# Four edits to a planned attention-and-FFN kernel: the first q in two parts, new delays in the planner, a second recursion level in one more block, and the last stores on two queues

## The chip, the cores and the metric

The kernel runs on one core of a Trainium2 chip. The core has five engines that run their own instruction streams in order: TensorE (PE; its weight loads are listed as PEld), VectorE (DVE), ScalarE (ACT), GpSimd (POOL) and SyncE (SP, which here only issues DMAs). They meet through semaphores. A DMA is issued by a queue on SP or ACT and its data is moved by the core's 16 DMA engines. The metric is device microseconds for one execution, lower is better. Before the change three runs gave a median of 1555.18 us, from 1553.32 to 1555.87.

## The reference

Two blocks in a row, all in float32 but for the FFN's weights, which arrive as float64:

```python
# attention: q, k, v are (batch 8, heads 12, seq 448, head_dim 64)
q_n, k_n = rmsnorm(q, g_q), rmsnorm(k, g_k)      # x / sqrt(mean(x*x) + 1e-6) * g
attn = softmax(q_n @ k_n.T / sqrt(64))
x = (attn @ v)  ->  reshaped to (3584, 768)      # token rows, heads side by side
# FFN: w_a, w_b are (768, 1536), w_out is (1536, 768)
out = ((x @ w_a) * (x @ w_b)) @ w_out            # (3584, 768)
```

## The kernel before

**Attention.** The work goes in 24 "couples" (`p`), each four heads of one batch entry, two and two on the halves of the 128 partitions. For a couple the kernel loads q, k and v (`loads`, L422; each as two DMAs of 224 KB on SP, one for each half), squares q and k on ScalarE (L456), sums the squares on VectorE (L458), scales them (L462) and takes the power -0.5 on GpSimd (L464), multiplies q by its root (`apply`, L468, tile `qn`), and turns k and q with TensorE transposes into one PSUM tile each (L494), which ScalarE copies out (L499 for k, L501 for q, times the gains). Then, over seven key blocks `j`, it makes scores (L515), exponentials (L521, two instructions a block, with k's root as the scale) and values (L537). The sum of exponentials is made by TensorE for the first five couples (L573) and by VectorE and GpSimd for the others (L551). Its reciprocal goes out to DRAM and back to be spread (`few`, `inv`, `rec`), and VectorE multiplies it in (L644).

**FFN.** The batch is taken in four blocks of two entries (`beta` 0 to 3). Each of the three products is done in Strassen's form with seven products in place of eight (the program's seven factors of a weight tile, `st`). The first two FFN products are `quarter_products` (L984, PSUM tile `pq`), the last one `last_product`, which handles pairs of 128-token tiles: three pairs in an even block, four in an odd one, and for each of seven products `f`, in the order 0, 1, 2, 4, 3, 5, 6, one TensorE product per pair (L726, tile `po`, 384 columns wide). In the fourth block alone (`ONCE = NB - 1`), and for five of the seven `f` (`TWICE`), two pairs at a time are done with a second level of the same recursion instead (`inner_products`): VectorE makes four sums of the left side (tile `Si`, L877), seven products of 192 columns go into five PSUM banks named a, b, d, g, e (L901), and small VectorE instructions of 192 or 384 columns put them together (L936 to L959). The right side's four extra factors are computed by VectorE in the second block (`inner_factors`, `MAKE = 1`, L840, tile `tk`), stored to DRAM (`kept_t`), and loaded again by `stream_inner` (tile `ti`, L856) into buffers that attention used: the four `ET` buffers, or the two of v and the one each of q and k. That load waits until the last couple has ended. Output rows are stored by `store` (L1056), two DMAs of 96 KB for 128 rows, all on SP; quarters of the second level first live in tiles `oi`, which take buffers of the nine-buffer pool `x`.

**Weights.** The float64 weights come in as words (`hraw`, `lraw`; `factors`, `rounding`, L379 loads on ACT) and are rounded to float32 by one ScalarE instruction (L271) and six VectorE ones, from which the seven factors are made, kept in DRAM, and loaded again for each later block (`stream`, L413 and L415). The first weight load is planned after the first k has arrived.

**What sets the order.** The class `Plan` collects every step with an engine, a cost in us, a priority key (smaller goes first), and what it reads and writes; tiles have a number of buffers. `run` simulates the engines with these costs, takes at each moment the ready step with the smallest key, and emits the instructions in that order. So each engine's program order is the planner's, and at run time an engine waits in that order. A step's result is available to another engine `LAG` = 0.1 us after its planned end. A DMA costs its size at 300 KB per us on one shared lane plus 2 us. TensorE has eight filler steps of warm-up (`warm`, L1073, 64 records in all) with the largest key: they run when nothing else is ready.

## Time and profile before

The profiled execution took 1556.43 us, of which 1554.5 us are the span from its first to its last instruction. Matmuls in float32 are recorded as two instructions each.

| quantity | value |
|---|---|
| median of three runs | 1555.18 us |
| profiled execution, its span | 1556.43 us, 1554.5 us |
| TensorE busy | 1515.1 us, 97% of the span |
| VectorE, ScalarE, GpSimd busy | 767.6, 399.3, 314.1 us |
| HBM read and written | 160.83 MB, 41.85 MB |
| quarter products L984 | 763.4 us by summed durations |
| last product, first level, L726 | 204.8 us (from hT) and 105.5 us (from fin) |

The stages stand one after the other on the time axis: attention of the first two blocks up to 236 us, with the rounding of the weights and the start of the FFN mixed in; the FFN of the first block from 236; attention in bursts around 394 to 522 and 755 to 882; and from 1139 to 1163 the last couples. The last product of the third block runs from 1172.4 to 1253.7, that of the fourth from 1443.1 to 1547.1. In the table of stretches a row gives the length, then for each engine its busy time and number of records, the clock granted to TensorE as a share of full speed, the share of time that the DMA engines were busy, and GB/s. The chain of waits is followed back from the last instruction; each piece is named by what it was waiting on or doing.

### The profile page before, as it was taken

To read this page: it belongs to the slowest core of one execution; us is meant where nothing else is said; L and a number is where in the kernel's file an instruction comes from. 1 tells how busy PE (TensorE), PEld (TensorE's weight loads), DVE (VectorE), ACT (ScalarE), POOL (GpSimd) and SP (SyncE) were. 2 spreads that over 40 slices of the span, in tenths; PEclk is the share of its full clock that TensorE was granted. 3 is DMA by queue.
4 is the path that set the end of the run, shared out by engine and by line. 5 is a ranking of instruction groups with operands and counts; after the bars stand their busy time and mean duration, and the time that the engine had idled before them with its cause. 6 is when DMAs were issued, how large, how long until landed. Compare 5 with 4: busy or idle time off the path is not lost.

```text
span 1554.5 us, 17614 instructions
## 1 busy us (share of the span) xinstructions
PE 1515.1 (97%) x6894; PEld 811.3 (52%) x6894; DVE 767.6 (49%) x1088; ACT 399.3 (26%) x647; POOL 314.1 (20%) x166
## 2 busy tenths in 40 slices
PE   8998999999999999999999999999999999999998
PEld 6554344555444555555444455555545555555796
DVE  4887869888786412222376532222135212222583
ACT  4767761111567200000456400000040000000000
POOL 2426442111255200011244400001110001000000
PEclk9999999999999999999999999999999999999999
DMA  8798445554535551212246445221324432222343
GB/s 238 223 264 247 97 104 181 184 196 152 161 110 126 143 164 71 107 71 102 78 107 167 107 149 169 77 101 71 107 74 139 130 124 104 75 88 84 117 137 105
DMA packets 122527, 204.09 MB, mean 131 GB/s; under 512 B 57156, under 2 KB 105540, under 8 KB 112708
## 3 DMA queue, kind: packets, MB, share of 16 engines
q1 hardware_dynamic: 94692, 149.80, 32.9%
q10 hardware_dynamic: 27744, 53.09, 9.8%
q8 instruction: 56, 0.92, 0.3%
q14 instruction: 35, 0.29, 0.1%
HBM read 160.83 MB, written 41.85 MB: 130 GB/s over the span
## 4 chain that ended last, share of the span: by engine, by line
PE 88%; DMA 5%; DVE 3%; ACT 3%; issue 1%; SPq 0%; POOL 0%; ACTq 0%; DVEq 0%; POOLq 0%
PE pq L984 49%; PE po L726 19%; PE o L537 6%; PE sc L515 6%; PE pt L494 2%; PE su L573 2%; ACT ET L521 2%; PE g L901 1%; DMA k_sb<-in_k_dram 1%; DMA q_sb<-in_q_dram 1%; PE a L901 1%; DMA rec<-inv 1%; PE warm L1073 1%; DMA hraw<-in_moe_w_out_dram 1%; PE b L901 1%
## 5 line engine op out<-in xcount | busy, mean ns | idle before, releaser
L984 PE MATMUL pq<-x,st 128*128 128x448 f32 x2016 | 763.4, 540 | 0.0
L984 PEld LDWEIGHTS pq<-x,st 128*128 128x128 f32 x2016 | 381.2, 190 | 378.6 <-issue 370.1
L521 ACT ACTIVATE ET<-sc,ms 128x448 f32<-128x448 f32 x336 | 192.6, 634 | 91.6 <-PE sc L515 67.1
L726 PE MATMUL po<-st,hT 128*128 128x384 f32 x624 | 204.8, 487 | 0.0
L515 PE MATMUL sc<-qkT 64*64 64x448 f32 x1344 | 176.7, 546 | 18.7 <-ACT ET L521 10.5
L537 PE MATMUL o<-ET,v_sb 64*64 64x448 f32 x1344 | 185.7, 551 | 8.1 <-ACT ET L521 7.5
L464 POOL TENSOR_TENSOR ms<-ms,expo 128x14 f32<-128x14 f32 x48 | 146.0, 3046 | 206.4 <-DVE ms L462 201.8
L1032 POOL TENSOR_TENSOR hT<-hT,t 128x448 f32<-128x448 f32 x24 | 28.7, 1197 | 745.9 <-DVE t L1030 743.7
L726 PEld LDWEIGHTS po<-st,hT 128*128 128x128 f32 x624 | 117.9, 190 | 84.7 <-issue 3.6
L1006 ACT COPY hT<-pq 128x448 f32<-128x448 f32 x24 | 12.8, 532 | 436.1 <-PE pq L984 436.1
L515 PEld LDWEIGHTS sc<-qkT 64*64 64x64 f32 x1344 | 58.5, 133 | 95.6 <-issue 35.0
L551 POOL TENSOR_TENSOR sum<-sum,ET 128x896 f32<-128x896 f32 x38 | 81.4, 2141 | 127.2 <-ACT ET L521 84.5
L726 PE MATMUL po<-st,fin 128*128 128x384 f32 x312 | 105.5, 490 | 0.0
L537 PEld LDWEIGHTS o<-ET,v_sb 64*64 64x64 f32 x1344 | 60.6, 134 | 84.9 <-issue 37.5
L726 PEld LDWEIGHTS po<-st,fin 128*128 128x128 f32 x312 | 58.3, 190 | 46.6 <-issue 8.5
L551 DVE TENSOR_TENSOR sum<-sum,ET 128x896 f32<-128x896 f32 x57 | 62.3, 1094 | 38.4 <-POOL sum L551 33.2
L746 DVE TENSOR_TENSOR o_sb<-fin,po 128x384 f32<-128x384 f32 x44 | 24.4, 554 | 112.7 <-PE po L726 108.6
L1044 POOL TENSOR_TENSOR hT<-hT,t 128x448 f32<-128x448 f32 x48 | 57.8, 1206 | 51.1 <-DVE t L1041 47.5
L458 DVE TENSOR_REDUCE ms<-sq 128x14 f32<-128x896 f32 x48 | 51.8, 1078 | 24.8 <-ACT sq L456 24.7
L1037 DVE TENSOR_TENSOR hT<-U,pq 128x448 f32<-128x448 f32 x48 | 29.8, 621 | 66.2 <-PE pq L984 66.2
L1041 DVE TENSOR_TENSOR t<-U,pq 128x448 f32<-128x448 f32 x48 | 29.7, 619 | 61.6 <-PE pq L984 59.3
L1009 ACT COPY t<-pq 128x448 f32<-128x448 f32 x24 | 12.8, 533 | 176.0 <-PE pq L984 176.0
(109 smaller groups left out, 1141.7 us busy)
## 6 DMA issues: line engine op xcount, KB each, us to landing
st<-kept SPq DMA_DIRECT2D x36, 1344.0 KB
st<-kept_o SPq DMA_DIRECT2D x28, 1152.0 KB
kept<-st ACTq DMA_DIRECT2D x12, 1344.0 KB
q_sb<-in_q_dram SPq DMA_DIRECT2D x48, 224.0 KB
k_sb<-in_k_dram SPq DMA_DIRECT2D x48, 224.0 KB
v_sb<-in_v_dram SPq DMA_DIRECT2D x48, 224.0 KB
rec<-inv SPq DMA_DIRECT2D x48, 224.0 KB
lraw<-in_moe_w_a_dram ACTq DMA_DIRECT2D x12, 768.0 KB
```

What stands on the lines that cost most here:

```text
L458: op("DVE", 1.1, key, lambda: nc.vector.tensor_reduce(rs[p][:, s], xs["sq", nm, p], AX, ALU.add), [sq], [f"{ms}/{nm}"])
L464: lambda: nc.gpsimd.tensor_tensor(msf(), msf(), expo[:, 0:2 * NT * (b - a)], ALU.pow), [], names)
L494: nc.tensor.transpose(t[:, j * P:(j + 1) * P], x[:, j].rearrange("p h d -> p (h d)"), ident)
L515: nc.tensor.matmul(t[low_high[w], e, 0:S], lhsT=qkTs[p][low_high[e], 1, j * P + w * D:j * P + (w + 1) * D], rhs=qkTs[p][low_high[e], 0, w ...
L521: nc.scalar.activation(E[:, e], scs[p, j][:, e, 0:S], AF.Exp, scale=rs[p][:, 1, 2 * j + e:2 * j + e + 1])
L537: nc.tensor.matmul(os_[p][low_high[e], w, 0:S], lhsT=xs["v", p][low_high[w], e, j * D:(j + 1) * D], rhs=ETs[p, j][low_high[w], e], start=( ...
L551: two[e].tensor_tensor(sums[p], sums[p] if j > 1 else ETs[p, 0], ETs[p, j], ALU.add)
L573: nc.tensor.matmul(sus[p][w][low_high[e], :], lhsT=ones[low_high[w], :], rhs=x[low_high[w], e], start=first, stop=last)
L726: nc.tensor.matmul(held["po"][:, 0:HALF], lhsT=a[0]()[:, c], rhs=sts[beta, 12 + place_of[f]][:, c], start=(c == 0), stop=(c == MH - 1))
L901: nc.tensor.matmul(held[bank], lhsT=x()[:, c], rhs=y(c), start=(start and c == 0), stop=(stop and c == MI - 1), skip_group_check=True)
L984: nc.tensor.matmul(banks[bank][:, 0:S], lhsT=sts[at][:, f, c * P:(c + 1) * P], rhs=quads[x][:, c], start=(start and c == 0), stop=(stop an ...
L1044: lambda i=i, n=n, nm=nm: two[TIMES].tensor_tensor(C(i, n), C(i, n), held[nm], ALU.mult), [t], [hp[i]],
```

## The change

1. *First q in two parts.* `begin_first`, called ahead of all else, allocates the first q tile and loads its second half from ACT's queue; the planned load then issues only the first half on SP. `prepare_first` replaces q's part of `normalize` for couple 0: squares, sums, scaling, power and `apply` are done for four of the seven 64-wide groups and then for three. The turn and the take of q are split alike, and the power for k is split in two, on which the first four and the last three key blocks' exponentials wait separately.
2. *Delays.* `LAG` is 0.05 us, and 0.22 us where the producer is TensorE.
3. *Second level in the third block.* `TWICE` becomes a table: all seven `f` in block `NB - 2`, the five as before in `NB - 1`; `ONCE` is `NB - 2`. The extra factors are made for all seven `f`. In the third block the pairs 0 and 1 are one group and pair 2 stays at the first level; pairs that stay alone are now issued ahead of the groups. With `ONCE` lower, the third block's FFN steps are listed after the last couple's, and its N sums are made by quarter as hT gets ready.
4. *The tail.* In the very last group (fourth block, `f` = 6, second group) product e goes ahead of the last g; the last product goes to a bank of its own, h, and the quarter is summed in two steps. For `f` = 6 of the fourth block each quarter row's two stores go to SP and ACT in turn.

```diff
-    LAG = 0.1
+    LAG, LAG_PE = 0.05, 0.22
...
-                    ready[u] = max(ready[u], end[x] + (self.LAG if ops[u][0] != e else 0.0))
+                    ready[u] = max(ready[u], end[x] + ((self.LAG if e != "PE" else self.LAG_PE) if ops[u][0] != e else 0.0))
...
-        TWICE = (1, 2, 3, 4, 6)
+        TWICE = {NB - 2: (0, 1, 2, 3, 4, 5, 6), NB - 1: (1, 2, 3, 4, 6)}
         MAKE = 1
-        ONCE = NB - 1
+        ONCE = NB - 2
...
+        FIRST = "q", 0
+        PARTS = slice(0, NT // 2 + 1), slice(NT // 2 + 1, NT)
+
+        def begin_first():
+            x = xs[FIRST] = ld.tile([P, 2, NT * D], FP32, tag="q", name="q_sb", bufs=1)
+            nc.scalar.dma_start(x[low_high[1]], q[0, 2:4].rearrange("h (p j) d -> p h (j d)", j=NT))
+
+        def prepare_first():
+            ms, key, sq = tile_of("ms0", "ms", 3), -NORM, tile_of("sqq0", "sq", 1)
...
+            for c in range(2):
+                n = PARTS[c].stop - PARTS[c].start
...
+                op("ACT", 0.1 + 0.13 * n, key, square, ["q0"], [f"{sq}/{c}"], new=[sq] if c == 0 else [])
+                op("DVE", 0.1 + 0.145 * n, key, lambda c=c, r=r: nc.vector.tensor_reduce(
...
+                op("POOL", 0.4 + 0.32 * n, key, lambda c=c, r=r, n=n: nc.gpsimd.tensor_tensor(
...
+                op("DVE", 0.1 + 0.145 * n, key, apply, [f"{ms}/q{c}", "q0"], [f"{qn}/{c}"], new=[qn] if c == 0 else [], lock=True)
...
+                        op("PE", 0.11 * m, key, turn_part, [f"qn0/{c}"], [f"{pt}/{c}"], new=[pt] if c == 0 else [], mode="full")
+                        op("ACT", 0.1 + 0.145 * m, key, take_part, [f"{pt}/{c}", "gain"], [f"{qkT}/0"])
...
-            op("ACT", 1.12, p, exps, [sc, f"ms{p}/k"], [E], new=[E])
+            op("ACT", 1.12, p, exps, [sc, f"ms{p}/k" if p else f"ms0/k{int(j >= PARTS[1].start)}"], [E], new=[E])
...
-                if beta == MAKE and f in TWICE:
+                if beta == MAKE:
                     inner_factors(beta, f)
-                if beta >= ONCE and f in TWICE:
+                if f in TWICE.get(beta, ()):
                     stream_inner(beta, f)
...
-                twice = groups if f in TWICE else []
+                twice = groups if f in TWICE.get(beta, ()) else []
+                for t in pairs if not twice else alone:
+                    product(t, f, a(t), plain(t, base, to))
                 for g in twice:
                     inner_products(beta, key + place_of[f], f, g, a, base, to, acc, (c_, U_), out_place)
-                for t in pairs if not twice else alone:
-                    product(t, f, a(t), plain(t, base, to))
...
+            third = lambda: product("e", s(3), b_quarter(1, 1), [f"{S_}/3", st], True, True)
+            last = beta == NB - 1 and f == 6 and group[0]
+            if last:
+                third()
+            product("g", s(2), b_made(2), [f"{S_}/2", f"ti{beta}.{f}.2"], True, bool(last))
...
+            if last:
+
+                w = write(1, 0)
+                add(0.36, lambda: V.tensor_tensor(dest(1, 0), part(1), held["g"], ALU.add), [g, f"{t_}/1"], **w)
+                home_of["h"] = "mm", 2
+                bank_of["h"] = tile_of(f"h_{id_}", "mm", 2)
+            product("h" if last else "g", a11, b_made(3), nx1 + [f"ti{beta}.{f}.3"], bool(last), True)
...
+                if beta == NB - 1 and f == 6:
+
+                    op("ACT", 1.0, -1, lambda x=x, t=t: store(out_place(t, to[0]), to[1], o_of[x], (nc.sync, nc.scalar)), [o_[x]], [],
+                       kb=197, dmas=2)
+                    continue
...
-                nc.sync.dma_start(rows[j][p0:p0 + n, x * HALF:(x + 1) * HALF], o_sb[at:at + n])
+                queues[0].dma_start(rows[j][p0:p0 + n, x * HALF:(x + 1) * HALF], o_sb[at:at + n])
+                queues.reverse()
...
         with tc.manual_schedule():
+            begin_first()
             setup()
             plan.run()
```

## The prediction

> **What bounds the kernel now.** I read four views in this order: the table of engines, a table of stretches of the span, the chain of waits, and the rows of the last twelve microseconds. First the engine table and the stretches (columns: length, then busy time and count for PE, PEld, DVE, ACT, POOL, then granted TensorE clock, DMA share, GB/s).
>
> ```profile
> PE 1515.1 (97%) x6894; PEld 811.3 (52%) x6894; DVE 767.6 (49%) x1088; ACT 399.3 (26%) x647; POOL 314.1 (20%) x166
> ```
>
> ```profile
> 15.00:40.00 25.00, 20.86 (x178) 12.24 (x182) 13.96 (x16) 14.10 (x20) 6.57 (x2) 0.86 0.91 293
> 40.00:80.00 40.00, 36.82 (x355) 23.08 (x347) 34.03 (x41) 28.51 (x46) 17.08 (x6) 0.96 0.81 225
> 80.00:120.00 40.00, 36.24 (x345) 19.75 (x337) 33.61 (x40) 29.02 (x45) 8.61 (x3) 1.00 0.98 267
> 120.00:160.00 40.00, 34.52 (x304) 16.73 (x302) 31.41 (x39) 29.52 (x49) 27.93 (x10) 1.00 0.72 216
> 882.00:962.00 80.00, 80.00 (x249) 47.10 (x248) 31.62 (x58) 0.00 (x0) 0.05 (x1) 1.00 0.52 164
> 1173.00:1254.00 81.00, 81.00 (x253) 47.69 (x252) 31.02 (x48) 1.44 (x3) 1.13 (x1) 1.00 0.43 137
> 1459.00:1517.00 58.00, 56.00 (x334) 53.73 (x333) 44.69 (x102) 2.65 (x9) 0.00 (x0) 1.00 0.51 156
> ```
>
> TensorE is the bound. It is without a gap where only FFN work is left (882 to 962, 1173 to 1254), and idle almost only in the first 160 us: 4.1, 3.2, 3.8 and 5.5 us in the four rows shown. So two kinds of change count: fewer matmul columns in a stretch that is full, and fewer holes at both ends.
>
> The chain of waits names the first hole (start, length, what):
>
> ```profile
> 1.36 10.32 PE warm L1073 x64
> 11.68 0.76 PE pt L494 x7
> 12.45 0.32 PE pg L1065 x2
> 12.79 0.16 ACT gain L1068
> ...
> 13.24 9.73 DMA hraw<-in_moe_w_out_dram
> ...
> 24.52 0.95 ACT sq L456
> 25.47 0.54 ACT ET L521
> ...
> 26.05 2.29 PE o L537 x8
> ```
>
> The start is not held by the first q: the 64 warm-up records hold TensorE until 11.68, though qn was done at 11.66. Then ScalarE meets its first weight rounding (L271) in program order after only two of seven key blocks, and its words land at 22.97; the exponentials queue behind it. TensorE has nothing from 21.97 to 26.05, and the granted clock is 0.50 from 26 to 30 (0.64 and 0.65 in the two slices beside); eight records of su or sc take 1.5 us there, 0.75 after it.
>
> The last view is the tail (start, length, engine, operation):
>
> ```profile
> 1545.87 1.24 PE L901 MATMUL g<-ti,hT 128*128 128x192 f32 x6
> 1547.15 0.35 DVE L959 TENSOR_TENSOR oi<-pi,g 128x192 f32<-128x192 f32 x1 [0.81 <-PE g L901]
> ...
> 1547.57 1.59 SPq L1056 DMA_DIRECT2D out_dram<-oi  x1
> ...
> 1549.21 0.59 SPq L1056 DMA_DIRECT2D out_dram<-oi  x1
> ```
>
> After the last sum, two stores leave one queue, one after the other; the second has left at 1549.80.
>
> **First q in two parts.** Loading one half by ACT removes one issue (0.72 us of SP's 1.44 us) ahead of q, k and the later loads. The squares, sums, roots and products are split 4 to 3: eight instructions more, some 0.1 to 0.4 us of fixed time each, on engines that idle there (DVE is busy 4.2 of the first 15 us). By themselves they gain nothing, because the warm-up, unchanged, still ends at 11.5 and the turn of k follows it. After it ScalarE has k's copy (0.91), then two takes for one (1.01 split, plus 0.1). Now the copy waits for the gain's copy, itself behind pg (12.45); if that order turns, scores start at 14.5 instead of 14.92: -0.4. What matters is the written order. With the planner's costs and transfer rate, by hand: the first exponential moves from 14.2 to 12.2, because apply needs 0.7 after a root of 1.7 instead of 1.15 after 2.7; the words' landing moves from about 17 to about 19, because their second issue falls behind the split takes and q's second load goes ahead. So some four key blocks and couple 1's squares stand ahead of the first rounding, not two. In real time a block takes 2.25 us, so TensorE has work to about 25 while the words still land near 23 to 24: the hole shrinks from 4.1 to 1 (-3.1), and with it goes the low clock, 2.7 us lost over 26 to 31.4. That is -6.2 by the time 32 us. Behind it lie DMA waits: a q load of 8.07 us on the chain at 66.15, and a reciprocal's return of 8.36 at 99.96, where DMA is busy 0.98. Work that is early there waits for the same bytes. I keep about half, -3.3. Ends: -7.5 (all, and a little of the next hole) and +3 (the same order puts another instruction behind a late transfer).
>
> [...]
>
> **Delays between engines (0.1 to 0.05, from TensorE 0.22).** No instruction is added; the order in the four attention bursts is made anew. What it can touch is the idle of TensorE there: 16 us between 40 and 236, 3.8 in 394 to 522, 3.1 in 755 to 882. Most of the first is DMA. I take -1, with ends of -6 and +6, since a list order can shift either way and nothing in this trace shows the new one.
>
> **Factors for two more products in the second block (f 0 and 5).** Per f eight VectorE subtractions (two each of 0.60, 0.56, 0.35 and 0.43: 3.9 us) and eight stores on SP (0.35 each). 882 to 962 has VectorE at 32 of 80 us: f 5 is hidden. f 0 comes in the burst of 800 to 882, where these subtractions already wait for their stores (5.7 us in five waits); the attention's sums and, on SP, the q, k and v loads queue behind. +0.5; ends 0 and +3.
>
> **Second level in the third block.** The 21 full products of 1172.4 to 1253.7 take 3.87 us each (48 records of four products last 15.48 us). A pair at the second level lasts 7.03 in the fourth block (1458.57 to 1465.60), against 7.74: -0.71, seven times, -5.0. Its cost: VectorE has four sums (0.55) and eight adds (0.35 to 0.56), 5.2 us instead of 1.1, so about 29 us more on 31 of 81; the fourth block runs at 45 of 58. There, one wait shows: TensorE 1.8 us (b, for Si) where sums between two products come first. The third block has the same place between f 2 and 4; the lone third pair, now first, covers 3.9 of some 5 us: +1.2. At the start VectorE stood 2.5 us for rec at 1184 and nothing needed it; now group f 0 queues behind: +1. DMA: 1152 KB more per f, some 100 GB/s on 137; 15 to 40 carried 293. The output quarters find two of nine x buffers, each free again some 10 us later. The block's N sums (L714, six of 0.95) move ahead into the quarter products. Sum -2.8. Ends: -5.0, and +4 if four and a half waits of 2 us arise.
>
> **Tail.** The e product goes ahead of the last g, the half of the last quarter is added before, so h no longer waits 0.22 for L953; each quarter's two stores leave by two queues. Last sum at 1546.98, ready 1547.33, issue 0.59 with 0.05 before: 1547.98 instead of 1549.80, -1.8. Ends -2.4 and 0 (the two queues hold each other).
>
> [...]
>
> **Sum.** -3.3 - 1.0 + 0.5 - 2.8 - 1.8 = -8.4 on the profiled execution's 1556.4 us (span 1554.5 and 1.9 around it). That run is 1.25 above the median of the runs, 1555.2; on the median it gives 1546.8, I say 1547.
>
> **The rivals.** No change can be told from measurement within 0.2%, 3.1 us: 1552.1 to 1558.3.
>
> *The start's gain is gone:* the warm-up holds TensorE and DMA fills 80 to 120 at 0.98, so what is early waits there. For it: the 8 us transfers on the chain. Against: the low clock is TensorE's own loss. Without the -3.3 and -1.0: 1551.
>
> *Start and second level both give nothing:* VectorE at some 60 of 76 us and takes in its queue eat the 5.0. For it: the wait for Si, in one of ten groups. Against: nine without. 1551 + 2.8 = 1554.
>
> *Everything lands:* -7.5 at the start, -4 from the order, -4.5 and -2: 1537. For it: 23 us of idle in the bursts. Against: DMA's share.
>
> *Slower:* an in-order engine is written behind a transfer that lands later than planned, as ScalarE behind the first words. The price of one is on record: 4.1 idle and 2.7 at low clock, 6.8. With the start's gain gone (1551), two new ones give 1564.7; it decides from 0.6 of one on, and counts as slower at 7.2 us, just over one. For it: the planner's flat 300 GB/s and 2 us of landing against a 9.73 us landing. Against: the stretches after 236 have little such idle.
>
> **How the numbers follow.** Forecast 0.42, everything lands 0.14, start gone 0.20 (0.14 of it below 1552.1), both gone 0.10 (0.03 below), slower 0.14 (0.11 above 1558.3). Faster 0.73, same 0.16, slower 0.11. The range 1538 to 1558 leaves out 0.11 above and some 0.07 below; the forecast's own range is 1543 to 1551.
>
> **What would show it.** Warm-up to 11.5 as before; the first rounding after about four key blocks; no idle of 4 us and clock 1.00 between 20 and 35. Between the last attention and the fourth block's first quarter product 76 to 79 us instead of 81.3. Last store left 0.6 us after the last sum. The forecast is wrong if a new hole of over 3 us stands in a burst, or if TensorE waits more than 4 us in all within the third block's last product.

## The result: no gain, 0.2% slower, and the profile after

The changed kernel took 1558.1 us (median of 4 runs, 1555.99 to 1559.45) beside 1555.08 us for the kernel before (4 runs, 1553.32 to 1555.87). The ratio is 1.0020 with a 95% interval of 1.0002 to 1.0037. The forecast was 1547.0 with a range from 1538 to 1558: the time lies just above the range, and the sign is the other one.

The profiled execution after took 1556.96 us, its span 1554.7 us; that of before 1556.43 and 1554.5. So the two profiled executions differ by 0.5 us only, the medians by 3.0; what follows explains the profiled pair, and 2.5 us of the difference of the medians lie in executions that no trace shows.

First the engine table and the stretches after, with the columns of the prediction's own tables.

```profile
PE 1513.3 (97%) x7020; PEld 827.9 (53%) x7020; DVE 812.8 (52%) x1182; ACT 403.2 (26%) x656; POOL 314.5 (20%) x168
```

```profile
15.00:40.00 25.00, 20.26 (x199) 12.57 (x199) 16.00 (x19) 17.94 (x28) 7.10 (x3) 1.00 1.02 283
40.00:80.00 40.00, 38.95 (x364) 24.89 (x364) 32.51 (x38) 28.09 (x44) 16.63 (x5) 0.96 0.74 217
80.00:120.00 40.00, 33.90 (x287) 17.51 (x287) 32.69 (x40) 24.46 (x38) 9.17 (x3) 0.96 0.90 239
120.00:160.00 40.00, 35.83 (x320) 16.53 (x313) 31.64 (x38) 31.09 (x50) 17.62 (x7) 1.00 0.84 233
1173.00:1254.00 81.00, 78.86 (x388) 64.08 (x388) 54.25 (x112) 5.81 (x13) 3.01 (x3) 1.00 0.71 234
1459.00:1517.00 58.00, 56.02 (x333) 53.57 (x332) 43.75 (x99) 3.05 (x9) 0.00 (x0) 1.00 0.46 149
```

The first rows show the start's story: in 15 to 40 more records and a full clock (0.86 before), and then 80 to 120 with 33.90 us of TensorE instead of 36.24. The row of the third block shows the second level: more records, VectorE from 31 to 54 us, 137 to 234 GB/s, and TensorE idle for 2.1 us where it had none.

Where the time went is read best from marks, the starts of the long unbroken pieces in the chain of waits. After:

```profile
575.63 178.14 PE pq L1075 x474
965.44 178.15 PE pq L1075 x474
1255.11 189.42 PE pq L1075 x504
```

The same three pieces start at 576.12, 961.16 and 1253.67 us before. Between them:

| stretch | before | after | difference |
|---|---|---|---|
| to the first piece | 576.12 | 575.63 | -0.5 |
| third burst (end of the first piece to the second) | 206.90 | 211.67 | +4.8 |
| last couples and third block's last product (end of the second piece to the third) | 114.37 | 111.52 | -2.85 |
| third piece to the last sum's start | 293.48 | 293.28 | -0.2 |
| last sum's start to the end of the span | 7.35 | 6.31 | -1.0 |

The sum is +0.2. One correction belongs to this table. A couple's turns (14 transposes, 0.98 + 0.93 us) moved from the stretch before the mark at 576 into the third burst. The groups of the third burst by line, operation and shape (count, busy us and mean ns of one), before and then after, show it:

```profile
L494 PE MATMUL pt<-ident,k_sb 128*128 128x128 f32 x35 | 4.8, 277 | 0.0
L494 PE MATMUL pt<-ident,qn 128*128 128x128 f32 x35 | 4.6, 273 | 0.0
```

```profile
L549 PE MATMUL pt<-ident,k_sb 128*128 128x128 f32 x42 | 5.8, 279 | 0.0
L549 PE MATMUL pt<-ident,qn 128*128 128x128 f32 x42 | 5.6, 274 | 0.0
```

These 1.9 us are neither won nor lost. Like for like the start became 1.4 us longer (575.63 + 1.9 against 576.12), and the third burst 2.9 us.

The start itself, as the timeline has it (start, length, engine, line, what; in brackets the wait before it and what ended it), two rows before and then after:

```profile
37.36 0.98 PE L494 MATMUL pt<-ident,k_sb 128*128 128x128 f32 x7
123.19 0.98 PE L494 MATMUL pt<-ident,k_sb 128*128 128x128 f32 x7
```

```profile
31.97 0.98 PE L549 MATMUL pt<-ident,k_sb 128*128 128x128 f32 x7
37.58 0.95 ACT L502 ACTIVATE sq<-q_sb 128x896 f32<-128x896 f32 x1 [2.77 <-DMA q_sb<-in_q_dram]
39.98 1.46 PE L609 MATMUL o<-ET,v_sb 64*64 64x448 f32 x5 [3.38 <-ACT ET L593]
113.84 0.95 ACT L502 ACTIVATE sq<-q_sb 128x896 f32<-128x896 f32 x1 [4.04 <-DMA q_sb<-in_q_dram]
115.36 1.54 PE L609 MATMUL o<-ET,v_sb 64*64 64x448 f32 x5 [2.19 <-ACT ET L593]
123.65 0.98 PE L549 MATMUL pt<-ident,k_sb 128*128 128x128 f32 x7
```

Couple 1's k is turned at 31.97 instead of 37.36: the predicted gain was there, 5.4 us of it. Then ScalarE's next instruction in written order is the square of a q that lands after 11.91 us on the chain (25.57 to 37.48), the exponentials stand behind that square, and TensorE stands for 3.38 us: the new hole of over 3 us that the prediction had named as a sign against it. The same happens at 110 to 114, with 2.19 us. The lead comes and goes between these places: the k of the next couples is turned 1.1 us earlier than before (55.13 against 56.26), 5.5 us (75.43 against 80.90), 1.5 us (99.84 against 101.37), and then 0.5 us later (123.65 against 123.19). So it is not lost at one place, and it is gone by 124.

The end of the span (VectorE's last sum, then the two stores):

```profile
1548.39 0.35 DVE L1043 TENSOR_TENSOR oi<-oi,h 128x192 f32<-128x192 f32 x1 [0.36 <-PE h L973]
1548.77 0.47 SPq L1148 DMA_DIRECT2D out_dram<-oi  x1
1548.77 0.50 ACTq L1148 DMA_DIRECT2D out_dram<-oi  x1
```

The stores have left 0.53 us after the last sum's end (1549.27 against 1548.74), as forecast; 5.4 us more pass before the span ends.

### The profile page after: what moved, and what is told of

Its sections match the earlier page's. It is cut to its first block, busy times and chain, and to the rows that moved or that the text cites. A ratio compares the mean times of both kernels' runs of the same rounds, so it can differ in the third digit from the quotient of the medians.

```text
span 1554.7 us, 18094 instructions
## 1 busy us (share of the span) xinstructions
PE 1513.3 (97%) x7020; PEld 827.9 (53%) x7020; DVE 812.8 (52%) x1182; ACT 403.2 (26%) x656; POOL 314.5 (20%) x168
## 4 chain that ended last, share of the span: by engine, by line
PE 86%; DVE 5%; DMA 4%; ACT 3%; issue 1%; POOL 1%; SPq 0%; ACTq 0%; DVEq 0%; POOLq 0%
PE pq L1075 48%; PE po L798 15%; PE o L609 6%; PE sc L587 6%; PE g L973 2%; DMA q_sb<-in_q_dram 2%; PE pt L549 2%; PE a L973 2%; PE su L645 2%; ACT ET L593 2%; PE b L973 1%; PE e L973 1%; PE d L973 1%; PE warm L1166 1%; DVE sum L623 1%
## 5 line engine op out<-in xcount | busy, mean ns | idle before, releaser
L510 POOL TENSOR_TENSOR ms<-ms,expo 128x14 f32<-128x14 f32 x46 | 139.9, 3044 | 227.3 <-DVE ms L508 218.6
L798 PE MATMUL po<-st,hT 128*128 128x384 f32 x504 | 166.3, 487 | 0.0
L798 PEld LDWEIGHTS po<-st,hT 128*128 128x128 f32 x504 | 95.0, 190 | 67.1 <-issue 3.6
L623 POOL TENSOR_TENSOR sum<-sum,ET 128x896 f32<-128x896 f32 x38 | 82.7, 2177 | 101.9 <-ACT ET L593 77.6
L798 PE MATMUL po<-st,fin 128*128 128x384 f32 x264 | 89.1, 489 | 0.0
L623 DVE TENSOR_TENSOR sum<-sum,ET 128x896 f32<-128x896 f32 x57 | 63.9, 1120 | 43.7 <-POOL sum L623 39.8
L798 PEld LDWEIGHTS po<-st,fin 128*128 128x128 f32 x264 | 49.4, 190 | 37.7 <-issue 5.6
L818 DVE TENSOR_TENSOR o_sb<-fin,po 128x384 f32<-128x384 f32 x36 | 20.0, 555 | 83.3 <-PE po L798 79.4
```

What stands on the lines that cost most here:

```text
L510: lambda: nc.gpsimd.tensor_tensor(msf(), msf(), expo[:, 0:2 * NT * (b - a)], ALU.pow), [], names)
L623: two[e].tensor_tensor(sums[p], sums[p] if j > 1 else ETs[p, 0], ETs[p, j], ALU.add)
L798: nc.tensor.matmul(held["po"][:, 0:HALF], lhsT=a[0]()[:, c], rhs=sts[beta, 12 + place_of[f]][:, c], start=(c == 0), stop=(c == MH - 1))
```

## The experiments

The theory from the two profiles: the parts that remake the order (the delays, the first q) put in-order engines behind transfers that land late, and this costs what the second level wins. Its rivals were that the second level itself pays in the third burst, that loads are late because the DMA engines are full, and that any new order of the first 250 us is a draw. "Before" is the kernel before, run beside each batch; its median there was 1555.8 to 1557.1 us.

| kernel | median us | ratio to before, 95% | first mark | third burst | to the third piece |
|---|---|---|---|---|---|
| before | 1555.1 | | 576.1 | 206.9 | 114.4 |
| after | 1558.1 | 1.0020 (1.0002 to 1.0037) | 575.6 | 211.7 | 111.5 |
| delays alone | 1573.9 | 1.0126 (1.0107 to 1.0145) | 588.0 | 211.9 | 114.4 |
| all but the delays | 1560.4 | 1.0022 (1.0011 to 1.0033) | 580.5 | 210.7 | 109.6 |
| first q alone | 1560.4 | 1.0034 (1.0022 to 1.0047) | 576.5 | 207.1 | 114.4 |
| second level alone | 1553.5 | 0.9983 (0.9971 to 0.9996) | 574.4 | 210.7 | 109.5 |
| second level without f 0 | 1553.7 | 0.9981 (0.9968 to 0.9994) | 577.8 | 208.2 | 112.2 |
| tail alone | 1556.3 | 0.9990 (0.9974 to 1.0005) | 574.4 | 207.7 | 114.4 |
| second level and tail | 1555.0 | 0.9983 (0.9970 to 0.9995) | 575.5 | 210.8 | 109.8 |

A mark is of one execution. Five of these kernels have one and the same written order up to 754 us at least (before, tail alone, and the three with the second level but neither the delays nor the first q), and their first marks lie from 574.4 to 577.8; first q alone and all but the delays share theirs up to 759 us, with marks of 576.5 and 580.5. So differences of under 4 us in the first mark mean nothing. In the third burst kernels of the same order agree better: 206.9 and 207.7 (before, tail alone), 210.7 and 210.8 (second level, without and with the tail).

**Each part by itself.** Delays alone:

```diff
-    LAG = 0.1
+    LAG, LAG_PE = 0.05, 0.22
```

> The kernel before with the new delays alone. Theory 1 (the order made with the new delays loses the 4.8 us by which the changed kernel is longer between the start of the attention burst at 754 us and the long last-product stretch after it, 132.1 against 127.4 us): that stretch takes 131 to 133 us here, and the kernel is 3 to 6 us slower than before. Theory 2 (the factors for f 0 and 5, made by VectorE in that burst, lose it): the stretch stays at 127 to 128 us and the time within 1.5 us of before.

Measured 1573.9 us, 1.3% slower. The stretch that the expectation names takes 132.4 us, as theory 1 said, but the loss of 18 us is far more than its 3 to 6, and it stands at the start, with a hole of 11 us. Stretches, and then the rows of ScalarE and TensorE at it; the last two rows are ScalarE's at the same place before:

```profile
88.00:92.00 4.00, 0.00 (x0) 0.00 (x0) 2.89 (x3) 0.00 (x0) 0.00 (x0) 0.81 1.13 321
92.00:96.00 4.00, 0.00 (x0) 0.00 (x0) 0.00 (x0) 0.76 (x1) 0.00 (x0) 0.50 1.08 340
96.00:100.00 4.00, 3.23 (x17) 2.10 (x21) 2.96 (x4) 3.13 (x6) 2.40 (x1) 0.50 0.39 145
```

```profile
95.24 0.95 ACT L456 ACTIVATE sq<-k_sb 128x896 f32<-128x896 f32 x1 [8.15 <-DMA k_sb<-in_k_dram]
96.77 2.29 PE L537 MATMUL o<-ET,v_sb 64*64 64x448 f32 x8 [11.24 <-ACT ET L521]
```

```profile
87.46 1.18 ACT L521 ACTIVATE ET<-sc,ms 128x448 f32<-128x448 f32 x2
88.50 0.97 ACT L456 ACTIVATE sq<-k_sb 128x896 f32<-128x896 f32 x1
```

At couple 3's turns and scores, 80.90 to 83.79, the two kernels stand at the same point to the hundredth of a microsecond. Then ScalarE's order differs: before, four exponentials stand ahead of the square of k; with the new delays the square stands first and waits for its load. Over 15 to 236 us TensorE is busy 13.5 us less (187.2 against 200.6).

All but the delays, in the changed kernel:

```diff
-    LAG, LAG_PE = 0.05, 0.22
+    LAG = 0.1
```

> The changed kernel with the old delay of 0.1 us everywhere, the other three parts kept. Theory 1: the burst is back at 127 to 128.5 us and the time is 1551 to 1554. Theory 2: the burst stays at 131 to 133 us and the time is within 1.5 us of the changed kernel.

1560.4 us. The delays cost 18 us by themselves and about nothing within the change: the parts do not add up. The burst is 1.0 us shorter than in the change, where theory 1 had it back near the old length. The second level is whole (109.6, from which one couple's turns have moved, as below). The start is 4.3 us later than before, which is hardly more than the scatter of the marks.

The second level alone:

```diff
-        TWICE = (1, 2, 3, 4, 6)
+        TWICE = {NB - 2: (0, 1, 2, 3, 4, 5, 6), NB - 1: (1, 2, 3, 4, 6)}
-        ONCE = NB - 1
+        ONCE = NB - 2
...
+                for t in pairs if not twice else alone:
+                    product(t, f, a(t), plain(t, base, to))
                 for g in twice:
```

> The kernel before with the second level in the third block alone (with the factors for f 0 and 5). Both theories: the third block's last product, from its first po to the next block's first quarter product, takes 78 to 79 us instead of 81.3. Theory 1: the burst before it stays at 127 to 128.5 us, the time is 2 to 3.5 us under before. Theory 2: the burst takes 131 to 133 us, the time is 1 to 3 us over before.

1553.5 us, better than before and than the change: the time is theory 1's, the longer burst theory 2's. Of the 4.9 us that the stretch to the third piece wins, 1.9 are one couple's turns, which moved from there into the third burst (42 + 42 of them as above, and none in the last couples' burst); 3.0 are the second level. Of the 3.8 us that the burst loses 1.9 are the same turns and 1.9 are new. Without the product whose factors are made in that burst:

```diff
+        TWICE = {NB - 2: (1, 2, 3, 4, 5, 6), NB - 1: (1, 2, 3, 4, 6)}
...
+                if beta == MAKE and f in TWICE[NB - 2]:
                     inner_factors(beta, f)
```

> The kernel before with the second level in the third block for six products, f 0 left at the first level, so that no extra factor is made for f 0 in the burst. Theory 2 (VectorE's factors for f 0, and the stores they wait for, lengthen the burst by 3.8 us, from the start of the long o row at 754 to the third block's first quarter products, 206.9 us before and 210.7 with all seven): that stretch is back at 206.5 to 208 us, the third block's last product saves 4.0 to 4.3 us, and the time is 3 to 5 us under before. Theory 1 (any new order in the burst loses): the stretch stays at 209 to 212 us and the time is within 1.5 us of before.

The burst comes down to 208.2 and the third block wins 2.2 instead of 3.0: f 0 costs in the burst (0.6 us) about what it wins later (0.8 us), both within the scatter of single executions, and the time is the same, 1553.7. Neither theory's numbers are met: 208.2 lies between their two stretches.

The first q alone (`begin_first`, `prepare_first` and the turns in two parts, as in the change):

```diff
+            else:
+                prepare_first()
...
+            begin_first()
             setup()
```

> The kernel before with the first q in two parts alone. Theory (the gain at the start is real and given back to the DMA): couple 1 is turned at 32 us instead of 37.4, a hole of 3 to 4 us with a low clock stands somewhere in 35 to 80 us behind a q load of 8 us or more, and the last product of the first block, at the 522 us mark, stands within 1.5 us of before. Rival (the prediction's term): the 522 us mark and the end are 3 us or more earlier.

and the tail alone:

```diff
+            last = beta == NB - 1 and f == 6 and group[0]
+            if last:
+                third()
...
+            product("h" if last else "g", a11, b_made(3), nx1 + [f"ti{beta}.{f}.3"], bool(last), True)
...
+                queues[0].dma_start(rows[j][p0:p0 + n, x * HALF:(x + 1) * HALF], o_sb[at:at + n])
+                queues.reverse()
```

> The kernel before with the tail's edits alone. The prediction's term: the time from the last sum's start to the end of the span goes from 7.35 us to 5.5, the whole 1.8 us down. Rival (the last landing does not care which queue issued it): last sum 0.2 us earlier, last sum to end 6.3 to 8 us, the whole within 1 us of before.

The first q alone is slower by 0.34%, though its profiled execution has the marks of before: with 1556.93 us that is the fastest of its twelve, and the trace of all but the delays, which has the same order at the start, has its mark 3.9 us later. Couple 1 is turned at 30.10 here, and a hole of 3.40 us follows, as the expectation said; but no load ends it. The exponentials wait for GpSimd's power for k:

```profile
38.20 0.63 ACT L593 ACTIVATE ET<-sc,ms 128x448 f32<-128x448 f32 x1 [2.78 <-POOL ms L510]
38.89 1.12 PE L609 MATMUL o<-ET,v_sb 64*64 64x448 f32 x5 [3.40 <-ACT ET L593]
```

The tail alone is not told from before; its time from the last sum's start to the end, 6.0 us, lies between the prediction's 5.5 and the rival's 6.3 to 8. Over all profiled executions of this study the time from the last sum's start to the end of the span is 6.7 to 7.8 us with the old tail (13 kernels, mean 7.3) and, with the new one, either 6.0 to 6.3 (four kernels) or 7.9 to 8.0 (three), mean 6.9.

**Is it the new delays, or any new order?** A number that nobody would call measured:

```diff
-    LAG = 0.1
+    LAG = 0.12
```

> The kernel before with a planner delay of 0.12 us in place of 0.1 for all engines, a change without a meaning. If the loss of 18 us by the new delays alone is what any new order can cost, this one too moves the time by 3 us or more, either way, with its holes in the first 250 us. If the values 0.05 and 0.22 themselves are what is wrong, it stays within 2 us of before.

1571.8 us (1.0103, 1.0086 to 1.0119), the first mark at 591.3. So it is not the two values of the new delays: 0.02 us more in the planner's one constant costs 15 us.

**Do the loads come late because DMA is full?** Eleven of the twelve stores of the first and second products' factors are left out, in the order of the new delays (later blocks then read the first tile's factors):

```diff
+                elif n:
+                    kept[n] = kept[0]
```

> The kernel before with the new delays alone, in the same written order, but 11 of the 12 stores of the factors of the first two weights (1344 KB each) are left out, and the later blocks read the first one's in their place; so less is moved in the first 250 us, and part of the computation is replaced. Theory (ScalarE stands in order behind a k load that lands late because the DMA engines are full): the hole of 11.2 us at 85 to 97 us shrinks below 5 us, and the time falls by 8 us or more from 1573.9. Rival (the order itself is bad whatever the transfers do): the hole stays above 8 us and the time falls by less than 4.

1575.4 us, the hole at 85 to 97 as large as before. This run tells little: the stores that it leaves out begin only behind the hole. So the load itself was made lighter, with 1792-byte pieces for 256-byte ones:

```diff
-    nc.sync.dma_start(x[low_high[w]], pair.rearrange("h (p j) d -> p j h d" if nm == "k" else "h (p j) d -> p h (j d)", j=NT))
+    to = x.rearrange("p j h d -> p (j h d)").rearrange("p (h n) -> p h n", h=2) if nm == "k" else x
+    nc.sync.dma_start(to[low_high[w]], pair.rearrange("h (p j) d -> p h (j d)", j=NT))
```

> The kernel before with one thing changed: k is loaded in pieces of 1792 bytes instead of 256 (the tile's layout no longer is k's, so the keys are mixed up and the attention it computes is another one; all instructions on the compute engines and their order stay). It is the base line for the next two. Theory D (in the first 250 us the engines wait for q and k loads that land late among other transfers): the many small pieces of k are the bulk of the packets, so the loads land earlier and the mark at 576 (start of the first block of quarter products of 576 us) comes 4 to 9 us earlier, time 1546 to 1551. Rival O (the written order itself costs the time, whatever the transfers do): mark within 1.5 us of 576.1, time within 3 us of 1555.

> The new delays alone (1573.9 us, mark 588.0, a hole of 11 us of TensorE at 85 to 97), with the same lighter load of k. Theory D: the square of k at 95 no longer waits 8 us, the hole at 85 to 97 shrinks under 4 us, and the mark at 576 comes within 4 us of the one with the lighter load and the old delays (it was 11.9 later); time within 5 us of that kernel. Rival O: the hole stays over 8 us and the mark stays 9 or more us behind; time 14 or more us above that kernel.

> The whole change with the same lighter load of k. Theory D (the first couple's gain of about 5 us is given back to late loads of q at 26 to 38 and 105 to 114): the mark at 576 is 3 to 7 us earlier than with the lighter load and the order of before, and the time 1 to 6 us below that kernel (the third burst still costs some 4, the third block and the tail win 4). Rival O (the new order gives it back whatever the loads do): mark within 1.5 us of that kernel's, time 0 to 3 us above it.

Measured 1554.5, 1570.2 and 1555.4 us, first marks 574.6, 585.4 and 575.5. Theory D missed in all three: the lighter load is worth 0 to 3 us at the mark, within the scatter, the delays still cost 10.8 us there, the whole change still has nothing. With the delays ScalarE's wait for k went from 8.15 to 5.51 us and the hole from 11.24 to 8.47. The DMA engines stayed as full in it (shares of 1.08 and 1.09 in 88 to 92 and 92 to 96, against 1.13 and 1.08 with the heavier load; 0.87 against 0.78 over 80 to 120). So it is not ruled out that full DMA engines make the loads late, with the 768 KB loads of the weights above all: no run made those smaller.

**Is it the place of one square on ScalarE?** The written order was changed by hand, after the planner, on ScalarE alone:

```diff
  ScalarE, kernel with the new delays
-L456 Activation sq<-k_sb 128x896
-L521 Activation ET<-sc,ms 128x448 x4
-L456 Activation sq<-q_sb 128x896
-L521 Activation ET<-sc,ms 128x448 x6
+L521 Activation ET<-sc,ms 128x448 x10
+L456 Activation sq<-k_sb 128x896
+L456 Activation sq<-q_sb 128x896
```

> The new delays alone, in the written order they give, with one thing moved by hand: on ScalarE, five key blocks' exponentials of couple 3 (ten instructions) go ahead of couple 4's square of k and the square of q behind it, for which ScalarE waited 8.15 us at 87 to 95; all other engines keep their order. Theory P (the place of the square in ScalarE's order costs the hole): the 11.24 us of TensorE's idle at 85 to 97 shrink to under 3, the low clock behind it goes, and the mark at 576 comes from 588.0 to 576 to 580; time 1562 to 1567 instead of 1573.9. Rival W (the loads set the pace; what is won is waited for later): mark 585 or more, time over 1570.

With two squares moved, and in the changed kernel three, the first of which is:

```diff
  ScalarE, kernel with the new delays, ahead of the edit above
-L456 Activation sq<-q_sb 128x896
 L499 TensorCopy qkT<-pt 128x896
 L521 Activation ET<-sc,ms 128x448 x2
 L501 Activation qkT<-pt,gain 128x896
+L521 Activation ET<-sc,ms 128x448 x4
+L456 Activation sq<-q_sb 128x896
...
-L521 Activation ET<-sc,ms 128x448 x2
 L400 DMACopy kept_o<-st 896x1x384
-L521 Activation ET<-sc,ms 128x448 x2
```

> The same, and also the square of couple 2's q (waited for 7.48 us at 28 to 36) moved behind the take of couple 1's k and three blocks' exponentials. Theory P: both holes go, 7.4 and 11.2 us and the low clock behind them; mark at 570 to 576, time 1556 to 1562. Rival W: mark within 2 us of the kernel with one move, time the same.

```diff
  ScalarE, changed kernel
-L502 Activation sq<-q_sb 128x896
 L705 TensorCopy x<-o 128x448 x2
-L593 Activation ET<-sc,ms 128x448 x2
+L593 Activation ET<-sc,ms 128x448 x6
+L502 Activation sq<-q_sb 128x896
 L400 DMACopy kept_o<-st 896x1x384
-L593 Activation ET<-sc,ms 128x448 x6
+L593 Activation ET<-sc,ms 128x448 x2
```

> The whole change with three squares of q moved on ScalarE, each behind three key blocks' exponentials that stood behind it (waits of 2.77 us at 35 to 38, 1.59 at 87 to 89, 4.04 at 110 to 114). Theory P: the two holes of TensorE at 36 to 40 and 112 to 116 go (3.4 and some 4 us with the low clock of 0.58 and 0.61 behind them, 2 us each by the clock in those rows): mark at 576 from 575.6 to 566 to 571, time 1549 to 1554. Rival W: mark 574 to 576, time 1556 to 1559, as the change itself.

Theory P fell, three times: 1575.9, 1575.0 and 1561.4 us, marks 590.9, 589.7 and 582.2. Rival W has the first two; the third is later than either theory had it. The hole did not go; it came in two pieces of the same sum. TensorE's rows with one square moved:

```profile
90.33 2.29 PE L537 MATMUL o<-ET,v_sb 64*64 64x448 f32 x8 [3.31 <-ACT ET L521]
112.95 2.29 PE L537 MATMUL o<-ET,v_sb 64*64 64x448 f32 x8 [8.03 <-ACT ET L521]
```

3.31 + 8.03 = 11.34, where one hole of 11.24 had been. The chain of waits of the same run shows what stands behind the first of them:

```profile
72.46 1.04 DVE st L392 x2
...
74.00 0.26 DVE few L606
74.27 5.97 DMA inv<-few
80.26 0.51 SPq L602
80.82 5.25 DMA rec<-inv
86.16 1.16 DVE x L644 x2
87.32 0.48 DVE st L392
...
89.00 0.52 ACTq L400
89.65 0.64 ACT ET L521
```

It is a loop over four queues: VectorE reaches the reciprocal (`few`) behind a weight's subtractions, its way through DRAM takes two landings of 5 to 6 us with SP's queue waiting in between, VectorE's multiply (L644) waits for that, the weight's next subtractions stand behind the multiply, their store stands ahead of the exponentials on ScalarE. By this reading a later square only lets ScalarE come sooner to the next of these waits.

In the changed kernel with three squares moved, the hole at 37 did go (23.45 us of TensorE in 15 to 40 instead of 20.26) and more than that came back in the next stretch, at a lower clock:

```profile
15.00:40.00 25.00, 23.45 (x229) 14.76 (x233) 14.63 (x16) 18.83 (x30) 7.05 (x2) 1.00 1.00 282
40.00:80.00 40.00, 32.56 (x293) 20.17 (x284) 29.34 (x36) 24.62 (x37) 16.84 (x5) 0.91 0.63 182
```

**Is it the reciprocals' way through DRAM?** One landing is taken out of the loop: nothing is stored, and the bytes that come back are read from q.

```diff
-    nc.sync.dma_start(fews[1].rearrange("e (p i) -> (e p) i", p=FEW), fews[0])
...
-    nc.sync.dma_start(sus[p][low_high[e]].rearrange("d w s -> d (w s)"), fews[1][e:e + 1, :].to_broadcast([D, 2 * S]))
+    nc.sync.dma_start(sus[p][low_high[e]].rearrange("d w s -> d (w s)"), q[0, 0:2].rearrange("h s d -> h (s d)")[e:e + 1, 0:2 * S].to_broadcast([D, 2 * S]))
```

> The kernel before, all instructions but one kind in their written order: the reciprocals are no longer stored to DRAM, and the 224 KB that come back for each couple are read from the input q instead (so what the outputs are multiplied with is not the reciprocal; the softmax's division is left out in effect). SP no longer waits for inv<-few (11.8 us in 40 to 125). Theory R (that way through DRAM paces the start): the mark at 576 comes 4 or more us earlier, time 1551 or less. Rival V (VectorE's queue and the loads pace it): mark within 2 us of 576.1, time 1553 to 1558.

> The same with the new delays alone. Theory R: in 1573.9 us the delays had put VectorE's reciprocal behind weight steps, so that SP's queue and the loads behind came late; without the landing of inv the hole at 85 to 97 falls from 11.2 to under 5 us, the mark comes from 588.0 to 577 to 582 and lies within 8 us of the kernel before with the same cut; time 1561 to 1567. Rival V: hole over 8 us, mark 11 or more us behind that kernel's, time over 1569.

Measured 1555.2 and 1571.9 us, marks 573.3 and 583.1. With the delays the hole halves:

```profile
91.88 2.29 PE L537 MATMUL o<-ET,v_sb 64*64 64x448 f32 x8 [5.97 <-ACT ET L521]
```

and the mark comes 4.9 us earlier; but 2.8 of these come without the delays too, and between the two orders 9.8 of the 11.9 us at the mark remain. The 2.8 and 4.9 us are within or near the scatter of the marks, the 9.8 are not. Neither theory has it whole: the landing is a link of the loop, and not what makes the difference between the two orders.

**Is it the planner's price of a landing?** One number in the changed kernel:

```diff
-    RATE, LANDING = 300.0, 2.0
+    RATE, LANDING = 300.0, 6.0
```

> The whole change with one number of the planner raised, the landing of a DMA from 2 to 6 us (the small ones of the chain take 5 to 6). If the low price is why the new orders stand behind late loads, the mark at 576 comes 4 to 9 us earlier than the change's 575.6 and the time is 1547 to 1553. If any new order of the first 250 us is a draw, the mark lies anywhere from 573 to 590, and the time from 1555 to 1575 is the likelier side, as four of the six re-planned starts so far lay later than the order of before.

1659.0 us, 6.6% slower than before, far outside what either reading expected. With landings nearer to the measured ones the planner wrote an order in which TensorE's own sums of exponentials wait for the reciprocals' return (ScalarE's L658 behind VectorE's multiply L716). TensorE's rows:

```profile
99.33 6.13 PE L645 MATMUL su<-ET,ones 64*64 64x448 f32 x32 [8.80 <-ACT rec L658]
138.47 5.34 PE L645 MATMUL su<-ET,ones 64*64 64x448 f32 x32 [15.57 <-ACT rec L658]
```

**The version that beats both.** The second level without the new delays and without the first q, here with the new tail (both edits as above):

> The kernel before with the second level in the third block and the new tail, without the new delays and the first q in two parts. Sum of the parts as they were measured alone: second level -1.6 us by median (third block -4.8, third burst +3.8), tail between -1.3 by its marks and +0.5 by median: 1552.3 us, 1550.5 to 1554; below the kernel before. If the parts were worth nothing beyond the scatter of the orders it would lie within 1 us of 1555 to 1556; if the order of the four parts together were what counts, above 1556.

1555.0 us, over the expected 1550.5 to 1554, beside 1556.8 for the kernel before in the same batch: 0.9983 of before, the same as the second level alone; both intervals lie below 1. By the ratio that is 2.6 us under the kernel before; against the change only the two ratios can be compared, 0.9983 and 1.0020.

## Why the prediction was wrong, step by step

- **What bounds the kernel, the first hole and its worth: right.** The step said that the hole of 4.1 us goes with its low clock and that this is worth 6.2 us by 32. Couple 1's turn came 5.4 us earlier and the clock of 15 to 40 is 1.00. The first rounding came after three key blocks, not some four, and its words had landed by 21.07 us, where the prediction had them at 23 to 24 still. The smaller term fell out: the scores start at 15.15 us, not 14.5 (14.92 before).
- **"I keep about half, -3.3": the step that failed.** Nothing was kept at the mark. The prediction named the two reasons (work that is early waits for the same bytes; another instruction behind a late transfer) and priced them at half. The profiled mark is 0.5 us earlier, 1.4 us later without the turns that moved across it; 4.7 us of the miss are here. One trace cannot tell 1.4 us from nothing, but four together tell that the 3.3 us are not there: with the first q in two parts the marks, like for like, are 577.5 (the change), 577.4 (the change with the lighter load of k), 576.5 and 580.5, mean 578.0; the five kernels with the old order have 574.4 to 577.8, mean 575.7. The rival "the start's gain is gone" describes this part.
- **"Delays -1, ends -6 and +6": failed in its bounds.** Alone the delays cost 18 us, and 0.02 us in the same constant cost 15. The prediction bounded a new order by the idle that the trace shows, which bounds what can be won, not what can be lost. Within the change the longer third burst cannot be laid to one part: it is 211.9 with the delays alone, 210.7 in the change without them, 211.7 in the change. Less the moved turns that is +3.1, +1.9 and +2.9; the parts do not add up. For the 2.9, -1 and, for the factors, +0.5 had been set: 3.4 us of the miss. Of the 2.9, 1.6 are TensorE waiting for VectorE's sum (L623 after), its other waits there are 0.2 us shorter (2.9 instead of 3.1), and 1.5 are longer busy time over the same matmuls (207.2 us instead of 203.8, less the turns).
- **Factors for f 0 and 5, +0.5: inside its ends.** With the old delays the burst grew by 1.9 us beyond the turns, by 1.3 with f 0 left out; within the change nothing is added to what the delays alone cost. One reading behind the term was off: the 5.7 us in five waits for stores are those of the whole second block. Between 800 and 882 us there are 1.8 us in two such waits, and 2.5 us in two waits for the load of `st`.
- **Second level -2.8: right in size, -2.85, the tenth by luck**; it is -3.0 alone. VectorE grew by 23 us where 29 were forecast, the traffic by 97 GB/s where 100 were. The prediction took off 2.2 us for a wait for the sums `Si` and a late start; neither came. In their place TensorE's last group waited 1.9 us for a quarter's buffer, behind a store of 8.14 us. In the kernel with three squares moved, with TensorE's order the same, that wait is not there and the stretch takes 109.7 us, 4.7 under before; in that with the lighter load of k the wait is 1.0 and the stretch 110.6. So the saving of columns is some 4.7 us, near the 5.0 forecast, and what a store's landing takes back varies from one execution to another. The waits and the chain after:

```profile
PE g L973 <- DVE oi L1029: 1.9, 1, 1.9
```

```profile
1243.50 8.14 DMA out_dram<-oi
1253.86 1.24 PE g L973 x6
```

- **Tail -1.8: right for the issue, wrong for the end.** From the last sum's start to the last store's departure there were 2.65 us, now 0.88: -1.77. The span won 1.0 of it, 1.2 with what product h won. On this pair the stretch behind the departure took up the rest: 4.70 us from there to the end of the span before, 5.43 after. Over all kernels the mean gain is 0.45 us. The issue is what was saved here; the forecast went by the issue rows, 1.59 and 0.59 us, and took what follows them as unchanged.
- **The sum:** 4.7 (start) + 3.4 (delays and factors in the third burst) + 0.6 (tail) - 0.1 (second level) = 8.6, from -8.4 to +0.2 on the profiled pair. The other 2.5 us between the forecast of 1547.0 and 1558.1 lie in executions that no trace shows.

The rival on the slower side named the mechanism that the start shows, an in-order engine written behind a transfer that lands later than planned. But the moved squares show that its price, 6.8 us for each, is no price of a place: a wait that is taken out comes back at the next one. That the places are links of one loop is read from the chains of waits, not shown by a run that opens it. What stays open is why the order of before loses 12 us less in this loop than that with the new delays. The size of k's loads, the place of the squares and one landing of the reciprocals were each tried, and each left 9 us or more of it; smaller loads of the weights were not.

## What to carry to other kernels

A stretch in which transfers, two in-order queues and a planner's order all meet cannot be priced by its idle: the idle bounds the gain of a new order but not its loss, so put a change that remakes the order to the test by itself, beside a change of the same constant that means nothing. An edit that only takes matmul columns out of a full stretch is priced well from the rows of a like stretch, here 4.7 us for a forecast of 5.0; the waits that it brings are not. Before reading a mark of one execution, look at the same mark in kernels whose order up to it is the same: here they differ by up to 4 us. Before reading a difference between two marks, count by shape what stands between them: here 1.9 us of transposes had changed places.

## What the hardware showed that was not expected

- **Half the clock after a hole of 2.19 us, the full clock after one of 2.52 us.** After the change TensorE stood from 113.17 to 115.36, and the granted clock was then 0.50 in the three rows from 116 to 119. In the kernel with three squares moved it stood from 144.85 to 147.37, and the rows from 145 to 151 have a clock of 1.00. Rows of both, after the change and then with three squares moved:

```profile
113.00:114.00 1.00, 0.17 (x3) 0.00 (x0) 0.00 (x0) 0.16 (x1) 1.00 (x1) 1.00 1.06 396
114.00:115.00 1.00, 0.00 (x0) 0.00 (x0) 0.53 (x2) 1.00 (x2) 0.49 (x1) 1.00 1.07 404
115.00:116.00 1.00, 0.64 (x5) 0.30 (x9) 1.00 (x1) 1.00 (x3) 0.00 (x0) 0.87 0.51 168
116.00:117.00 1.00, 1.00 (x9) 0.54 (x11) 0.96 (x2) 0.89 (x2) 0.00 (x0) 0.50 0.05 17
117.00:118.00 1.00, 1.00 (x8) 0.35 (x4) 1.00 (x1) 0.00 (x0) 0.00 (x0) 0.50 0.00 0
118.00:119.00 1.00, 1.00 (x12) 0.53 (x8) 0.97 (x3) 0.00 (x0) 0.00 (x0) 0.50 0.12 50
```

```profile
145.00:148.00 3.00, 0.63 (x6) 0.63 (x7) 1.62 (x4) 3.00 (x6) 3.00 (x2) 1.00 1.02 373
148.00:151.00 3.00, 2.93 (x31) 1.64 (x33) 1.09 (x1) 2.28 (x3) 3.00 (x2) 1.00 0.99 381
```

  So of these two holes the shorter one has the low clock behind it. What decides between them was not shown by any run.
- **The last stores land in two ways.** Behind the new tail the span ends 6.0 to 6.3 or 7.9 to 8.0 us after the last sum's start, with the same issues at the same places, and with nothing between in seven kernels. No run here shows why.
- **7 KB took 5.97 us to land in one place and 1.36 us in another.** The 7 KB of reciprocals took 5.97 us to land on the chain at 74.27 with one square moved, and 1.36 us at 97.07 in the change with three squares moved; the 224 KB that come back took 3.38 us (at 123.73) and 6.78 us (at 99.42) there. The planner has one number, 2 us, for all of them, and a larger one, 6 us, made the kernel 6.6% slower than before (1659.0 us).
